# Products of 512 columns in place of two of 256, in the first superblock and the single feature tile of an MLP

## The chip, the cores and the metric

The kernel runs on one core of a Trainium2 chip. The metric is the device time of one execution in microseconds (us). The kernel before has a median of 372.47 us over three runs.

## The reference

One block of a network on x of shape 2048 x 512 (float32), with six modulation rows made from a condition vector c:

```python
mod = (silu(c) @ w_mod).reshape(6, 512)
sa, ca, ga, sb, cb, gb = mod
h = layernorm(x) * (1 + ca) + sa
x = x + ga * irfft2(rfft2(h) * (w_r + 1j * w_i))
h = layernorm(x) * (1 + cb) + sb
act = mish(h @ w1 + b1)              # w1: 512 x 1376
x = x + gb * (act @ w2)              # w2: 1376 x 512
```

## The kernel before

The Fourier filter is done first, as products with matrices of the transform: phase 1 forward (L258, L303 to L305, to 50 us), phase 2 with the filter (L528 to L597, to 90 us), and phase 3, the inverse, in 16 steps, each a `p3_col` (L830 and L831) and a `p3_row` (L840, with its add to x in L843), from 90.4 to 150 us. The weights of the MLP are prepared beside it, and the MLP starts at 133 us, while the last rows are added.

The MLP takes the 2048 rows in four superblocks `i` of 512, each made of two blocks `b` of 256. The 1376 features are five tiles of 256 (`t` = 1 to 5) and a single tile of 96 (`t` = 0, `FL` = 96). A float32 operand is split into a high and a low part, so that one product is three products of the list `TERMS` (high by high, high by low, low by high). `up` (L942) multiplies a block of the first weights, 2 x 2 blocks `A11` to `A22` to a tile, by an input block `B11` to `B22` (`Bkj`: contraction half k, row block j of the superblock); ScalarE evicts the result with Mish. In superblocks 1 to 3 the products are those of a scheme of seven products for 2 x 2 blocks (`PRODUCTS`), which needs sums of the blocks (`sum_w1`, L747, split by `split_w1`, L726 and L727). In superblock 0, the `PLAIN` one, they are the eight direct products, each of 6 instructions of 256 columns. `up_single` (L991) is the first product of the single tile, `down` the second product (L1041 for t = 0, L1045 for the others), `halves` splits the results for it (L877 on ScalarE, L878 on VectorE), `last_down` (L1057) is the end of the last block. `load_w1` (L716) loads both halves of a tile's first weights, `split_in` (L821, L822) splits an input block, `sum_w2` (L874) and `split_w2` (L877, L878) prepare the second weights, `mod_second` (L619) loads a piece of the modulation weights and `mod_column` (L165) sums it on VectorE.

The split input blocks live in tiles called slots: B11 and B21 in tiles of their own, B12 and B22 in a tile `hcr` in the space (tag `cr`) of a constant of the inverse transform, free after the last `p3_col`.

From phase 3 on every step stands in a plan with a key, and the plan is run in the order of a table of numbers, `ORDER`, in which the steps are named by their rank by key. Each engine takes its instructions in that order, and waits at the head of its queue; DMAs go out from SP's queue in the same way.

Of the kernel before, what the change touches and what calls it, by code (L numbers as in the profile page):

```python
# [82 lines left out]
def tile_spectral_block(ctx: ExitStack, tc: tile.TileContext, x_d, w1_d, b1_d, w2_d,  # L83
# [614 lines left out]
    odd = [pm.tile([P, 512], F32, name=f"odd{i}") for i in range(4)]  # L698
    slots = {b: pm.tile([P, 2, 2, 256], F32R, name=f"h{b}") for b in ("B11", "B21")}
# [206 lines left out]
    def hold(b, t):  # L906
        raw[b, t] = next(turn[b % 2])
        return raw[b, t]
# [18 lines left out]
    def up(i, t, j):  # L927
        a, b = j if (i, t) in PLAIN else PRODUCTS[j]
        w, h = ring[t, a], slots[b]
        if (i, t) in PLAIN:  # L930
            at, half = plain_place(t, int(a[1]) - 1, int(b[2]) - 1)
            if (i, t, at) not in ups:
                ups[i, t, at] = bank("AD"[at])
            o = ups[i, t, at][:, 256 * half:256 * half + 256]
            first, last = a[2] == "1" and half == 0, a[2] == "2"
        else:
            o = region(i, t, j)
            first, last = j in (1, 5), True
        n = 0
        for p, q in TERMS:  # L940
            for k in range(2):
                nc.tensor.matmul(o, w[:, p, k, :], h[:, q, k, :], start=(first and n == 0), stop=(last and n == 5),  # L942
                                 skip_group_check=True)
                n += 1
# [39 lines left out]
    def up_single(i, u):  # L984
        if u == 0:
            ups[i, 0] = bank("D")
        s = u // 2
        o = ups[i, 0][:FL, 256 * s:256 * s + 256]
        for m in range(6 * (u % 2), 6 * (u % 2) + 6):
            (p, q), k = TERMS[m // 4], m % 4  # L990
            nc.tensor.matmul(o, w1s[:, p, k, :], slots[f"B{k // 2 + 1}{s + 1}"][:, q, k % 2, :],  # L991
                             start=(u == 0 and m == 0), stop=(m == 11), skip_group_check=True)
# [32 lines left out]
    def order(b, t):  # L1025
        if t == 0:
            return [(n, half, d) for n, half in ((1, 1), (2, 0)) for d in range(2)]
# [4 lines left out]
    def down(b, t, c):  # L1032
# [5 lines left out]
        for i, (p, q) in enumerate(TERMS):  # L1038
            if t == 0:
                n, half, d = piece  # L1040
                nc.tensor.matmul(out_ps[b][n][:, 256 * d:256 * d + 256], a[p][:FL, half],  # L1041
                                 w2[0][q][:FL, 256 * d:256 * d + 256], start=False, stop=False, skip_group_check=True)
# [133 lines left out]
    def late_slots():  # L1176
        cr = big.tile([P, 2, 2, 2, 256], F32R, name="hcr", tag="cr")
        slots["B12"], slots["B22"] = cr[:, 0], cr[:, 1]

    plan.at(-0.95, late_slots)  # L1180
# [17 lines left out]
    first_odd = odd[1]  # L1198

    def odd_space():  # L1200
        odd[:] = [buf("g1"), buf("g1")] + odd
# [281 lines left out]
```

## Time and profile before

| | |
|---|---|
| time, median of three runs (lowest to highest) | 372.47 us (372.26 to 372.69) |
| the profiled execution | 372.4 us |
| its span, first to last instruction | 370.5 us |
| mean granted TensorE clock | 0.997 |
| PE busy, matmuls | 363.6 us (98%), 2884 |
| VectorE busy | 309.9 us (84%) |
| ScalarE busy | 253.6 us (68%) |
| GpSimd busy | 64.8 us (17%) |

The profiled execution's own time is 1.9 us above its span, which is what lies around the instructions. Matmuls are pipelined, so the duration of one (283 ns for 256 columns) is longer than the interval at which they follow one another; a cost is read from the start of one to the start of the next.

### The profile page before, as it was taken

Reading aid. Unit: us, or ns where it says so; the run is one execution under the profiler, and the core shown is the slowest. Engines: PE = TensorE matmul, PEld = TensorE weight load, DVE = VectorE, ACT = ScalarE, POOL = GpSimd, SP = SyncE. Lnnn points to the kernel's source line nnn. Section 1 sums busy time; section 2 is a strip of 40 time slices with the busy share of each in tenths; the row PEclk is TensorE's granted clock in tenths of the full one; section 3 lists DMA queues with packets and bytes.
Section 4 is the critical chain, followed back from the end, with each engine's and each line's share of the span. In section 5 each row is a group of like instructions: output and inputs, shape, how many; then the busy total and the mean of one; then the engine's idle time right before and its main releaser. Section 6 shows DMA issues by size and latency. Waiting matters only on the chain.

```text
span 370.5 us, 8169 instructions
## 1 busy us (share of the span) xinstructions
PE 363.6 (98%) x2884; PEld 348.6 (94%) x2884; DVE 309.9 (84%) x760; ACT 253.6 (68%) x553; POOL 64.8 (17%) x102
## 2 busy tenths in 40 slices
PE   8999999998999999999999999999999999999995
PEld 8989977777999999999999999999999999999994
DVE  1898967888898899999898868996768978867896
ACT  1698879996557789789575778765686744555750
POOL 0478738786000000000001000000000000000000
PEclk9999999999999999999999999999999999999998
DMA  7999998777624656856978699775996797936032
GB/s 233 380 340 350 346 389 264 239 177 288 230 85 143 227 193 226 284 178 222 316 237 219 199 282 271 238 211 168 291 303 224 196 306 227 296 121 176 15 58 113
DMA packets 50888, 85.79 MB, mean 232 GB/s; under 512 B 7169, under 2 KB 18529, under 8 KB 50593
## 3 DMA queue, kind: packets, MB, share of 16 engines
q1 hardware_dynamic: 47680, 74.65, 60.2%
q10 hardware_dynamic: 2160, 6.95, 6.0%
q0 software_dynamic: 1008, 3.67, 5.9%
q8 instruction: 23, 0.38, 0.4%
q14 instruction: 17, 0.13, 0.1%
HBM read 66.12 MB, written 15.47 MB: 220 GB/s over the span
## 4 chain that ended last, share of the span: by engine, by line
PE 84%; DVE 7%; ACT 5%; issue 2%; ACTq 1%; POOL 0%; DVEq 0%
PE bank L942 28%; PE bank L1045 24%; PE bank L830 4%; PE bank L840 4%; PE bank L831 4%; PE bank L258 4%; PE bank L991 3%; PE bank L303 3%; PE bank L1041 3%; ACT buf L580 1%; PE bank L314 1%; PE bank L305 1%; PE bank L304 1%; ACT buf L579 1%; ACT d L441 1%
## 5 line engine op out<-in xcount | busy, mean ns | idle before, releaser
L1097 POOL DMA_DIRECT2D x<-modr x7 | 6.2, 888 | 260.2 <-DVE st L172 104.5
L942 PE MATMUL bank<-hT,wr 128*128 128x256 f32 x360 | 51.7, 283 | 0.0
L942 PEld LDWEIGHTS bank<-hT,wr 128*128 128x128 f32 x360 | 46.9, 192 | 0.1
L942 PE MATMUL bank<-hB,wr 128*128 128x256 f32 x300 | 43.4, 284 | 0.0
L942 PEld LDWEIGHTS bank<-hB,wr 128*128 128x128 f32 x300 | 39.1, 191 | 0.0
L1045 PE MATMUL bank<-w2a,ah 128*128 128x256 f32 x161 | 35.3, 283 | 0.0
L878 DVE TENSOR_TENSOR al<-buf,ah 128x512 fp32r<-128x512 f32 (+1 forms) x45 | 29.7, 666 | 4.6 <-ACT ah L877 4.5
L1045 PE MATMUL bank<-w2b,ah 128*128 128x256 f32 x147 | 32.3, 283 | 0.0
L877 ACT CAST ah<-buf 128x512 fp32r<-128x512 f32 (+1 forms) x45 | 26.9, 602 | 5.6 <-PE bank L1045 3.2
L942 PE MATMUL bank<-hcr,wr 128*128 128x256 f32 x210 | 30.0, 283 | 0.0
L942 PEld LDWEIGHTS bank<-hcr,wr 128*128 128x128 f32 x210 | 27.2, 192 | 0.0
L1045 PEld LDWEIGHTS bank<-w2a,ah 128*128 128x128 f32 x161 | 26.8, 192 | 0.0
L830 PE MATMUL bank<-kc,d 128*128 128x128 f32 x128 | 24.9, 276 | 0.5 <-ACT d L441 0.5
L831 PE MATMUL bank<-kc,d 128*128 128x128 f32 x128 | 24.7, 275 | 0.0
L1045 PEld LDWEIGHTS bank<-w2b,ah 128*128 128x128 f32 x147 | 24.6, 191 | 0.0
L1045 PE MATMUL bank<-w,ah 128*128 128x256 f32 x112 | 22.0, 286 | 0.0
L172 DVE BATCH_NORM_STATS2 st<-x 128x6 f32<-128x512 f32 x32 | 21.9, 685 | 0.0
L303 PE MATMUL bank<-buf,mring 128*128 128x512 f32 x48 | 20.6, 430 | 0.2 <-DVE buf L296 0.2
L830 PEld LDWEIGHTS bank<-kc,d 128*128 128x128 f32 x128 | 19.4, 192 | 0.7 <-ACT d L441 0.7
L831 PEld LDWEIGHTS bank<-kc,d 128*128 128x128 f32 x128 | 19.4, 192 | 0.0
L597 PEld LDWEIGHTS bank<-kv,a_sb 128*128 128x128 f32 x126 | 15.4, 191 | 2.7 <-issue 2.2
L833 ACT COPY buf<-bank 128x512 f32<-128x512 f32 x16 | 9.3, 583 | 12.5 <-PE bank L831 12.5
(295 smaller groups left out, 1099.1 us busy)
## 6 DMA issues: line engine op xcount, KB each, us to landing
wr<-w_S SPq DMA_DIRECT2D x60, 256.0 KB, 3.7
wr<-w_A SPq DMA_DIRECT2D x45, 256.0 KB, 4.1
w_S<-hT SPq DMA_DIRECT2D x20, 256.0 KB, 2.0
x<-in_A_x_dram SPq DMA_DIRECT2D x16, 256.0 KB, 5.1
xring<-in_x_t_dram SPq DMA_DIRECT2D x16, 256.0 KB, 5.0
w_A<-wr SPq DMA_DIRECT2D x15, 256.0 KB, 2.6
x<-modr POOLq DMA_DIRECT2D x7, 512.0 KB, 5.6
out_dram<-x SPq DMA_DIRECT2D x7, 512.0 KB, 3.8
```

The source lines that it names most:

```text
L172: nc.vector.bn_stats(t, x[:, n, :])
L258: nc.tensor.matmul(pgv[:, j], data(j), krs[:, j, :].rearrange("p (c q) -> p c q", c=2), start=True, stop=True)
L303: nc.tensor.matmul(pa, m[:, a, 0:128], g, start=(i == 0), stop=False)
L597: nc.tensor.matmul(pd[:, i * P:(i + 1) * P], y[:, i * P:(i + 1) * P], kv[:, 0:128], start=True, stop=True)
L830: nc.tensor.matmul(o, dj[:, 0:128], kc[0][:, n, :], start=True, stop=False)
L831: nc.tensor.matmul(o, dj[:, 64:192], kc[1][:, n, :], start=False, stop=True)
L840: nc.tensor.matmul(px[:, j * P:(j + 1) * P], e[:, j * P:(j + 1) * P], kiv[:, j, :], start=True, stop=True)
L877: nc.scalar.copy(h, r)
L878: nc.vector.tensor_tensor(l, r, plain(h), op=ALU.subtract)
L942: nc.tensor.matmul(o, w[:, p, k, :], h[:, q, k, :], start=(first and n == 0), stop=(last and n == 5), skip_group_check=True)
L991: nc.tensor.matmul(o, w1s[:, p, k, :], slots[f"B{k // 2 + 1}{s + 1}"][:, q, k % 2, :], start=(u == 0 and m == 0), stop=(m == 11), skip_gro ...
L1045: nc.tensor.matmul(out_ps[b][n][:, 256 * half:256 * half + 256], a[p][:, e], w2[t][q][:, r], start=(t == 1 and half == 0 and i == 0), stop ...
```

## The change

In superblock 0, the tiles t = 2 to 5 are multiplied by a weight block with both row blocks at once: three instructions of 512 columns for one half of the contraction of a weight block (`b` in `up` is that half), where there were two times three of 256. The moving operand is then two runs of 256 columns, from the new paired tiles `sides`, which hold Bk1 and Bk2 side by side. The single tile does the same in `up_single`, in all four superblocks, and its second product (`down` with t = 0, blocks 0 to 6) writes the 512 output columns with one instruction. B12 and B22 thus move out of `hcr` into `sides`; four of the tiles for results of odd blocks (`odd`) move into the space `cr` instead. `ORDER` is written anew (1155 steps where there were 1170).

```diff
 ORDER = (
-    "3 1 0 2 5 16 21 52 6 15 7 32 8 10 4 12 17 13 11 14 73 24 19 38 47 26 9 22 75 62 23 71 27 20 69 118 18 25 29 "
...
+    "3-4 1-2 16 0 21 15 9 71 5 73 32 75 80 7 10 12 14 8 17 13 82 26 19 6 38 47 11 22 124 23-24 85 20 18 29 51 27 62 "
...
-    odd = [pm.tile([P, 512], F32, name=f"odd{i}") for i in range(4)]
-    slots = {b: pm.tile([P, 2, 2, 256], F32R, name=f"h{b}") for b in ("B11", "B21")}
+    odd = []
+    sides = [pm.tile([P, 2, 2, 2, 256], F32R, name=f"hB{k}") for k in (1, 2)]
+    slots = {f"B{k + 1}{s + 1}": sides[k][:, s] for k in range(2) for s in range(2)}
...
     def hold(b, t):
-        raw[b, t] = next(turn[b % 2])
+        n = next(turn[b % 2])
+        raw[b, t] = odd[n if b % 2 else 3] if b % 2 or n < 0 else (even[2], even[1], even[0], scb)[n]
         return raw[b, t]
...
     def up(i, t, j):
         a, b = j if (i, t) in PLAIN else PRODUCTS[j]
+        if (i, t) in PLAIN and t > 1:
+            f = int(a[1]) - 1
+            if (i, t, f) not in ups:
+                ups[i, t, f] = bank("AD"[f])
+            for n, (p, q) in enumerate(TERMS):
+                nc.tensor.matmul(ups[i, t, f], ring[t, a][:, p, b, :], sides[int(a[2]) - 1][:, :, q, b, :],
+                                 start=(a[2] == "1" and b == 0 and n == 0), stop=(a[2] == "2" and b == 1 and n == 2),
+                                 skip_group_check=True)
+            return
...
     def up_single(i, u):
         if u == 0:
             ups[i, 0] = bank("D")
-        s = u // 2
-        o = ups[i, 0][:FL, 256 * s:256 * s + 256]
-        for m in range(6 * (u % 2), 6 * (u % 2) + 6):
-            (p, q), k = TERMS[m // 4], m % 4
-            nc.tensor.matmul(o, w1s[:, p, k, :], slots[f"B{k // 2 + 1}{s + 1}"][:, q, k % 2, :],
-                             start=(u == 0 and m == 0), stop=(m == 11), skip_group_check=True)
+        for p, q in TERMS:
+            nc.tensor.matmul(ups[i, 0][:FL], w1s[:, p, u, :], sides[u // 2][:, :, q, u % 2, :],
+                             start=(u == 0 and p + q == 0), stop=(u == 3 and p == 1), skip_group_check=True)
...
         if t == 0:
-            return [(n, half, d) for n, half in ((1, 1), (2, 0)) for d in range(2)]
+            return [(1, 1), (2, 0)]
...
             if t == 0:
-                n, half, d = piece
-                nc.tensor.matmul(out_ps[b][n][:, 256 * d:256 * d + 256], a[p][:FL, half],
-                                 w2[0][q][:FL, 256 * d:256 * d + 256], start=False, stop=False, skip_group_check=True)
+                n, half = piece
+                nc.tensor.matmul(out_ps[b][n], a[p][:FL, half], w2[0][q][:FL], start=False, stop=False,
+                                 skip_group_check=True)
...
-    def late_slots():
-        cr = big.tile([P, 2, 2, 2, 256], F32R, name="hcr", tag="cr")
-        slots["B12"], slots["B22"] = cr[:, 0], cr[:, 1]
-
-    plan.at(-0.95, late_slots)
...
-    first_odd = odd[1]
-
     def odd_space():
-        odd[:] = [buf("g1"), buf("g1")] + odd
+        late = big.tile([P, 4, 512], F32, name="odd", tag="cr")
+        odd[:] = [buf("g1"), buf("g1")] + [late[:, i] for i in range(4)]
...
-    BY_WEIGHT = pairs("111", "112", "121", "122", "211", "212", "221", "222")
+    BY_WEIGHT = [(a, k) for a in ("A11", "A12", "A21", "A22") for k in range(2)]
...
-            for c in range(n):
-                plan.at(key + 0.5 * c, down, b, t, c)
-            key += 0.5 * n
+                plan.at(key + (0.5 if t else 1) * c, down, b, t, c)
+            key += 0.5 * n if t else 2
```

The code above the changed functions is one line shorter now, so L942's place for the direct products is L952 for t = 1 and L935 for t = 2 to 5, and L840's is unchanged.

TensorE's queue at the start of the MLP before (`hB_1287` and `hB_1288` are B11 and B21, `hcr` is B12 or B22, `wr` a weight block, L840 a `p3_row`):

```order
L942 MATMUL bank<-hB_1287,wr 128x256 x6
L942 MATMUL bank<-hB_1288,wr 128x256 x6
L840 MATMUL bank<-kiv,buf 128x128 x4
L942 MATMUL bank<-hB_1287,wr 128x256 x6
L942 MATMUL bank<-hcr,wr 128x256 x12
L942 MATMUL bank<-hB_1287,wr 128x256 x12
L942 MATMUL bank<-hB_1288,wr 128x256 x6
L942 MATMUL bank<-hcr,wr 128x256 x6
L942 MATMUL bank<-hB_1288,wr 128x256 x6
L942 MATMUL bank<-hcr,wr 128x256 x24
```

The same place after (`hB_1283` holds B11 and B12, `hB_1284` B21 and B22):

```order
L952 MATMUL bank<-hB_1283,wr 128x256 x6
L952 MATMUL bank<-hB_1284,wr 128x256 x6
L952 MATMUL bank<-hB_1283,wr 128x256 x6
L952 MATMUL bank<-hB_1284,wr 128x256 x6
L952 MATMUL bank<-hB_1283,wr 128x256 x6
L840 MATMUL bank<-kiv,buf 128x128 x4
L935 MATMUL bank<-hB_1283,wr 128x512 x3
L952 MATMUL bank<-hB_1284,wr 128x256 x6
```

Of t = 1 the order goes A11 B11, A12 B21, A21 B11, A22 B21, A11 B12, A12 B22; the first product with B22 is at the start of the 24 in the last row before, and is the last row after.

VectorE's queue at the start of phase 3, between the sums of the second weights (L874) and the first norms, before (`w_1241` and `w_1242` hold the second weights of t = 1, `modr` their sums, `hT_1358` the loaded first weights of t = 1):

```order
L165 SCALAR_TENSOR_TENSOR buf,cols<-buf,bank 128x512
L878 TENSOR_TENSOR w_1242<-buf,w_1241 128x256
L878 TENSOR_TENSOR w_1242<-buf,w_1241 128x512
L843 TENSOR_TENSOR x<-x,bank 128x512
L878 TENSOR_TENSOR w_1242<-modr,w_1241 128x1024
L172 BN_STATS st<-x 128x6
L173 BN_AGGR mv<-st 128x2
L843 TENSOR_TENSOR x<-x,bank 128x512
```

And after (`hT_1292` is the loaded weights, `hT_1321` their sums, `hT_1322` the split sums):

```order
L878 TENSOR_TENSOR w_1242<-buf,w_1241 128x256
L878 TENSOR_TENSOR w_1242<-buf,w_1241 128x512
L747 TENSOR_TENSOR hT_1321<-hT_1292 128x256 x2
L878 TENSOR_TENSOR w_1242<-modr,w_1241 128x1024
L727 TENSOR_TENSOR hT_1322<-hT_1321,hT_1322 128x256 x2
L843 TENSOR_TENSOR x<-x,bank 128x512 x2
L171 BN_STATS st<-x 128x6
```

Two sums of first weights and the splits of their low parts now stand ahead of the first two adds of phase 3, and the third column sum of the modulation (L165, now L164) has moved behind them.

SP's queue of DMAs there, before:

```order
L866 DMA buf<-in_B_w_dram 128x512 x2
L619 DMA buf<-in_w_mod_dram 128x512 x5
L716 DMA hT_1358<-in_B_w_dram 128x4x256
L716 DMA hT_1381<-in_B_w_dram 128x4x256
L866 DMA buf<-in_B_w_dram 128x512 x2
```

And after:

```order
L866 DMA buf<-in_B_w_dram 128x512 x2
L618 DMA buf<-in_w_mod_dram 128x512 x2
L716 DMA hT_1292<-in_B_w_dram 128x4x256
L618 DMA buf<-in_w_mod_dram 128x512 x2
L757 DMA buf<-in_B_w_dram 128x4x96
```

The first load of the first weights went ahead of three of the five pieces of the modulation's, and the second load of them behind.

More of the change, by code (lines that the diff above doesn't have):

```diff
@@ L1196, in tile_spectral_block @@
             plan.at(key + scale * at, sum_w1, t, a, step)
-    first_odd = odd[1]
     def odd_space():
-        odd[:] = [buf("g1"), buf("g1")] + odd
+        late = big.tile([P, 4, 512], F32, name="odd", tag="cr")
+        odd[:] = [buf("g1"), buf("g1")] + [late[:, i] for i in range(4)]
     plan.at(1.6, odd_space)
-    turn = turns([even[2], first_odd, even[1], even[0], scb], [even[2], even[1], even[0], scb]), turns([], odd)
+    turn = turns([0, -1, 1, 2, 3], range(4)), turns([], range(6))
     def pairs(*ab):
@@ L1231, in tile_spectral_block @@
         if (i, t) in PLAIN:
-            f, e = int(j[0][1]) - 1, int(j[1][2]) - 1
-            at, half = plain_place(t, f, e)
-            if j[0][2] == "2" and half:
+            f, e = int(j[0][1]) - 1, int(j[1][2]) - 1 if t == 1 else j[1]
+            if j[0][2] == "2" and (f if t == 1 else e):
                 for h in range(2):
@@ L1291, in tile_spectral_block @@
                 plan.at(u + s + 2, scale_turned, b, g)
-        split_at, sum_at = (((35.2, 36.2, 37.2, 38, 37.5, 38.7, 40, 40.5), (35.4, 38.2, 36.5, 39.2)) if i == 1 else
+        split_at, sum_at = (((36.6, 36.8, 38.3, 38, 37.5, 38.7, 40, 40.5), (36.9, 38.2, 37, 39.2)) if i == 1 else
                             ((33.3, 33.8, 37.3, 38.3, 39.3, 40.3, 41.3, 42.3), (34.65, 35.15, 36.65, 38.15)))
```

85 rows, old and new, of the table ORDER are left out of this document.

## The prediction, made before the changed kernel was run

> **What bounds the kernel now.** I read the page first, for the engines' shares, then the busy time by stretches, the waits of TensorE, the chain that ended last, and the timeline of single engines where the change touches them.
>
> ```profile
> PE 363.6 (98%) x2884; PEld 348.6 (94%) x2884; DVE 309.9 (84%) x760; ACT 253.6 (68%) x553; POOL 64.8 (17%) x102
> PE bank L942 28%; PE bank L1045 24%; PE bank L830 4%; PE bank L840 4%; PE bank L831 4%; PE bank L258 4%; PE bank L991 3%; PE bank L303 3%; PE bank L1041 3%; ACT buf L580 1%; PE bank L314 1%; PE bank L305 1%; PE bank L304 1%; ACT buf L579 1%; ACT d L441 1%
> ```
>
> TensorE is busy for 98% of the span, and the products of the MLP (L942, L1045, L991, L1041) are most of the chain that ended last. The busy time by stretches (columns: the stretch, its length, PE, PEld, DVE, ACT, POOL, granted clock, DMA share, GB/s) says it stage by stage:
>
> ```profile
> 96.00:133.30 37.30, 37.30 (x337) 37.30 (x336) 34.84 (x86) 24.82 (x55) 0.00 (x0) 1.00 0.52 177
> 133.30:180.00 46.70, 46.70 (x395) 46.70 (x394) 43.78 (x117) 39.16 (x89) 0.00 (x0) 1.00 0.69 235
> 100.00:340.00 240.00, 240.00 (x2027) 239.98 (x2026) 204.98 (x513) 164.46 (x352) 5.37 (x6) 1.00 0.73 226
> ```
>
> From 100 to 340 us TensorE never stops, at a granted clock of 1.00. VectorE is at 93% and 94% in the two early stretches, so it is the engine that may become late. The waits of TensorE (us in total, times, longest), the one wait of its weight loads at the end, and the last wait of VectorE for TensorE:
>
> ```profile
> PE bank L830 <- ACT d L441: 0.5, 1, 0.5
> 356.84 0.19 PEld L1057 LDWEIGHTS bank<-w2hi,al 128*128 128x128 f32 x1 [0.24 <-DVE al L878]
> 344.86 0.42 DVE L978 TENSOR_TENSOR buf<-buf,bank 128x256 f32<-128x256 f32 x1 [0.47 <-PE bank L942]
> ```
>
> The first is at 90.4 us, at the start of the inverse transform; the second comes when nearly all is done. VectorE itself last waits for TensorE at 344.86, so an earlier TensorE pulls the tail with it: time taken out of TensorE's queue before that point is time off the end, unless something else is late.
>
> **The change part by part: what is saved.** 186 pairs of products of 256 columns become single products of 512: in the first superblock t=2 to 5 have 4 x 8 units of 6 products, 192, now 96 (96 pairs); the single tile's first product has 4 x 24, now 4 x 12 (48 pairs); its second has 7 blocks x 12, now 6 (42 pairs). The columns streamed stay the same; what goes is a fixed part for each product. Its size is the interval from one product's start to the next, in the chain (start, length, what) and in the timeline at the end, where products of 512 already run:
>
> ```profile
> 135.87 12.22 PE bank L942 x102
> 205.38 1.44 PE bank L1041 x12
> 220.84 1.42 PE bank L991 x12
> 360.75 0.63 PE L1057 MATMUL bank<-w2b,ah 128*128 128x512 f32 x2
> 361.22 0.39 PE L1057 MATMUL bank<-w2b,al 128*128 128x512 f32 x1
> 361.45 0.63 PE L1057 MATMUL bank<-w2b,ah 128*128 128x512 f32 x2
> 361.91 0.39 PE L1057 MATMUL bank<-w2b,al 128*128 128x512 f32 x1
> 362.14 0.39 PE L1057 MATMUL bank<-w2c,ah 128*128 128x512 f32 x1
> ```
>
> A product of 256 takes 12.22 / 102 = 120 ns in the first product, 1.44 / 12 = 120 in the second, 1.42 / 12 = 118 in the single tile's first. Six of 512 go from 360.75 to 362.14: 1.39 / 6 = 231 or 232 ns; I take 231. A pair saves 240 - 231 = 9 ns, or 236.5 - 231 = 5.5 with the single tile's weights of 96 columns. The sum: 96 x 9 = 0.86 us, 42 x 9 = 0.38, 48 x 5.5 = 0.26, together 1.5 us. All of it lies on the path, since TensorE is never idle there, but for some 3 pairs that follow 344.86 (0.03 us).
>
> The bounds of this come from phase 1, where both sizes alternate:
>
> ```profile
> 26.51 0.40 PE L303 MATMUL bank<-buf,mring 128*128 128x512 f32 x1
> 26.75 0.28 PE L304 MATMUL bank<-buf,mring 128*128 128x256 f32 x1
> 26.86 0.28 PE L305 MATMUL bank<-buf,mring 128*128 128x256 f32 x1
> 26.98 0.40 PE L303 MATMUL bank<-buf,mring 128*128 128x512 f32 x1
> ```
>
> Here 512 columns take 0.24 and two of 256 take 0.23: no saving at all to the second digit. That is the low end, 0: the same columns stream, and nothing in these rows makes one long product dearer than two short ones. The high end is 186 x 11 = 2.0 us, if the 512 runs at 229 (361.45, 361.91 and 362.14 lie 0.23 to a product apart, read to the second digit). I take 9, since those rows have the MLP's own tiles and the other kind of row has weights in another order. The fixed part left by these rows is 240 - 231 = 9 ns for each product. The Trainium skill, TensorE: Matmul & The Clock Gate, section Back-to-back issue gap, gives an isolated gap of columns / 2.4 plus 2.5 ns, 215.8 for 512 and 109.2 for 256; the trace has 231 and 120, so it does not agree in size. By that rule a pair would save 2.6 ns and the whole change 0.5 us.
>
> **What is moved.** The content of every other engine's queue stays: the same casts, subtractions and transfers, in another order. Three places decide whether TensorE runs into a wait.
>
> First, the low part of B22 (L822), which VectorE makes just before TensorE multiplies with it:
>
> ```profile
> 139.67 0.69 DVE L822 TENSOR_TENSOR hcr<-even,hcr 128x512 fp32r<-128x512 f32 x1
> 140.28 0.42 DVE L727 TENSOR_TENSOR hT<-wsum,hT 128x256 fp32r<-128x256 f32 x1
> 92.65 0.42 DVE L874 TENSOR_TENSOR modr<-buf 128x256 f32<-128x256 f32 x1
> 92.99 0.42 DVE L874 TENSOR_TENSOR modr<-buf,modr 128x256 f32<-128x256 f32 x1
> ```
>
> The two L874 rows show an operation on 256 columns at 0.34 from start to start (92.65 to 92.99), the first two rows one on 512 at 0.61. The low part ends at 139.67 + 0.69 = 140.36; TensorE gets to that block 48 products after 135.87, at 141.62, 1.26 us later. After the change TensorE gets there with 30 products of 256 fewer in front (3.60 us) and 3 of 512 more (0.69): 2.91 us sooner. VectorE has less ahead of it too: three differences of weights (L747) and two of L874 move behind it, 0.34 each, 1.70; one split of 256 and one of 512 of the second weights move behind, 0.34 + 0.61; a column sum for the gate moves ahead (+0.61) and one p3_row add behind (-0.61), both on 512. Together 2.65 us. The slack becomes 1.26 - (2.91 - 2.65) = 1.0 us: still no wait.
>
> Second, the start of the inverse transform. The load of the first pair of weight blocks (L716, 512 KB) moves in SP's queue ahead of three loads of the modulation (L619), and what VectorE makes of it moves ahead of the first two p3_row adds (L843): two differences (L747) and two splits (L727). Before:
>
> ```profile
> 84.46 11.24 SPq L619 DMA_DIRECT2D buf<-in_w_mod_dram  x5
> 95.89 0.93 SPq L716 DMA_DIRECT2D hT<-in_B_w_dram  x2
> hT<-in_B_w_dram SPq DMA_DIRECT2D x5, 512.0 KB, 4.2
> wm<-in_w_mod_dram SPq DMA_DIRECT2D x7, 256.0 KB, 8.8
> 89.18 0.68 DVE L165 SCALAR_TENSOR_TENSOR wm<-wm,bank 128x512 f32<-128x512 f32 x1
> 94.65 0.69 DVE L165 SCALAR_TENSOR_TENSOR buf<-buf,bank 128x512 f32<-128x512 f32 x1 [1.24 <-DMA buf<-in_w_mod_dram]
> 95.26 1.14 DVE L878 TENSOR_TENSOR w<-buf,w 128x256 fp32r<-128x256 f32 x2
> 96.32 0.68 DVE L843 TENSOR_TENSOR x<-x,bank 128x512 f32<-128x512 f32 x1
> 96.92 1.22 DVE L878 TENSOR_TENSOR w<-modr,w 128x1024 fp32r<-128x1024 f32 x1
> 98.06 0.69 DVE L172 BATCH_NORM_STATS2 st<-x 128x6 f32<-128x512 f32 x1
> 99.43 0.83 PE L840 MATMUL bank<-kiv,buf 128*128 128x128 f32 x6
> ```
>
> The load can go out once VectorE's second sum of wm is done, at 89.18 + 0.68 = 89.86, so about 89.9, and lands 4.2 us later by the median of its kind, at 94.1. VectorE, which now doesn't stand 1.24 us for the third modulation block, goes on from 92.99 + 0.34 = 93.33 with the splits of 256 and 512, 0.34 + 0.61, to 94.3, or 94.6 where it waits for ScalarE's casts, as it does between 95.26 and 96.32; then 0.67 (two differences), 1.14 (the split of 1024, 96.92 to 98.06), 0.67 (two splits of 256) and 0.60 (the add, 96.32 to 96.92) take the add to 97.7. TensorE wants the bank it frees for its third p3_row at 99.43. Slack 1.7 us: no wait; behind this add stand only row 1's add and the sums of the norm.
>
> Third, the tiles. B12 and B22 now share tiles with B11 and B21 and need not await the end of the inverse transform, and four tiles for odd blocks take over the old space; the first use of these comes with results of t=2, which TensorE makes after the last p3_col:
>
> ```profile
> 133.32 0.22 PE bank L831 x2
> ```
>
> That only relaxes the early part, and I cost it at nothing; its cover is the 12 us of products from 135.87 on, which follow in either kernel. If a first eviction did stand in ScalarE's queue there, its bank would be late for TensorE, and 0.04 of the chances below is kept for that. In superblocks 1 to 3 the steps keep their neighbours; TensorE loses 24 pairs' worth, 0.2 us, in each against VectorE, which has more than 30 us of idle time in 100 to 340. So I add nothing.
>
> The profiled execution took 372.4 us for a span of 370.5; the runs' median is 372.47. The sum is 370.5 - 1.5 = 369.0 of span, 1.9 around it, and 370.9 by the profiled time, 371.0 by the median. I say **371.0 us**. 0.2%, about what a measurement of this kernel can tell from no change, is 0.75 us.
>
> **The rivals.**
>
> *The load is late (slower).* At the start of the inverse transform the load of 512 KB could take the 8.8 us that the wm rows show in the same queue: it lands at 98.7, VectorE's queue stands, the add ends 98.7 + 0.67 + 1.14 + 0.67 + 0.60 = 101.8, and TensorE, wanting the bank at 99.43, waits 2.4 us: 371.0 + 2.4 = 373.4. It decides from a landing later than 99.43 - 3.08 = 96.35, 6.4 us after the issue. For it: the wm rows. Against it: all five loads of this very kind, median 4.2. Chance 0.12.
>
> *VectorE takes the gain at B22 (same).* If VectorE's queue is later by 1.0 us plus what is gained, TensorE waits for the low part of B22 and the end stays where VectorE puts it: 372.3. For it: 94% of VectorE in that stretch. Against it: the count above, with 1.0 us to spare. Chance 0.08.
>
> *The pairs save nothing (same).* If the moving operand in two runs of 256 costs as two products, or a product's fixed part is as in phase 1 (0.24 against 0.23), the time stays at 372.4. No row of before has a moving operand in two runs; for it stand the phase 1 rows, against it those of L1057. By that rule of the Trainium skill it would be 372.0. Chance 0.08.
>
> **How the numbers follow.** The forecast has 0.68: 371.0, or 370.4 to 371.7 with 2.0 us and 0.75 us for the gain. The late load has 0.12, and 0.04 I keep for a wait of its size elsewhere, such as that of the evictions for the new tiles; the two rivals in between 0.08 + 0.08 = 0.16. Faster by over 0.2% is the forecast's: 0.68. Within 0.2%: the two rivals, 0.16. Slower: 0.12 + 0.04 = 0.16. For 8 in 10 the forecast's own range and the rivals in between don't quite do, as some of the forecast's 0.68 lies outside 370.4 to 371.7; so the range reaches on to the late load's price: 370.4 to 373.4.
>
> **What would show it.** Right: TensorE's busy time shorter by about 1.5 us with 186 fewer products; products of 512 in L935 and in the single tile's lines at 231 ns from start to start; no new wait of PE between 91 and 356 us. The late load would show as a wait of PE L840 <- DVE x L843 near 99 us, with VectorE idle for a transfer to hT just before; the B22 rival as PE waiting for DVE L822 near 139; the third as 240 ns between products of 512. The forecast is wrong if the busy time of PE falls by under 0.75 us, or if it falls as said and idle time of the same size appears.

## The result and the profile after

The changed kernel is slower, by 1%:

| | before | after |
|---|---|---|
| median of five runs (lowest to highest) | 372.53 us (372.26 to 372.69) | 376.07 us (375.12 to 377.41) |
| ratio, 95% interval | | 1.0098 (1.0071 to 1.0126) |
| profiled execution | 372.4 us | 375.33 us |
| its span | 370.5 us | 373.2 us |
| matmuls | 2884 | 2698 |

The profiled execution of the changed kernel is one of the faster of its five.

The page of the changed kernel, busy time and the chain that ended last:

```profile
PE 362.7 (97%) x2698; PEld 338.0 (91%) x2698; DVE 309.5 (83%) x760; ACT 252.0 (68%) x553; POOL 64.9 (17%) x102
PE 88%; DVE 6%; DMA 3%; issue 1%; ACT 0%; SPq 0%; DVEq 0%; ACTq 0%
```

186 products are gone, yet the chain now has 3% of DMA in it, where the page of before names no DMA among the engines of its chain. The waits of TensorE name it (us in total, times, longest); no such row stood before:

```profile
PE bank L952 <- DMA wr<-w_S: 3.3, 1, 3.3
```

TensorE waited once, for 3.3 us, for a weight block fetched into `wr` (L952 makes the products of superblocks 1 to 3 too, not only those of t = 1). The chain around that moment (start, length, what):

```profile
254.04 5.71 DMA wr<-w_S
259.75 0.14 issue
259.89 1.37 PE bank L952 x6
261.26 1.28 PE bank L1052 x6
262.54 1.24 PE bank L1048 x3
```

The fetch was issued at 254.04 and landed 5.71 us later. SP's queue says why it went so late: its timeline after, and one of its waits between 240 and 262 us.

```profile
244.75 0.32 SPq L723 DMA_DIRECT2D wr<-w_S  x1
249.88 4.06 SPq L790 DMA_DIRECT2D turned<-x  x4
254.04 1.21 SPq L723 DMA_DIRECT2D wr<-w_S  x1
SPq L790 <- DVE x L784: 4.7, 1, 4.7
```

From about 245 us SP stood with `turn_out` of rows 12 and 13 (L790) at the head of its queue, 4.7 us, for a transpose of VectorE (L784). Its four DMAs then took 4.06 us to go out, and only then came the fetch of t=3 S3, which TensorE wanted at 256.6 (259.89 less its wait of 3.3). Before the change the same four DMAs stood behind that fetch and four more (S3 is the second `w_S` of the first row, A11 and A22 are the second row, S4 and S2 the third):

```profile
246.05 1.76 SPq L723 DMA_DIRECT2D wr<-w_S  x2
248.57 2.48 SPq L723 DMA_DIRECT2D wr<-w_A  x2
252.53 1.26 SPq L723 DMA_DIRECT2D wr<-w_S  x2
256.14 1.77 SPq L790 DMA_DIRECT2D turned<-x  x4
```

The loss is larger than the wait. The rows after it are slow: 6 products of 256 in 1.37 and in 1.28 us, 228 and 213 ns each where 120 is usual. The granted clock in the stretches before, in and after the wait (the column before the last two):

```profile
256.00:259.89 3.89, 0.60 (x6) 0.42 (x5) 1.06 (x5) 0.00 (x0) 0.00 (x0) 1.00 0.94 241
259.89:263.80 3.91, 3.91 (x17) 3.63 (x18) 0.89 (x2) 1.44 (x3) 0.00 (x0) 0.56 1.02 366
263.80:268.00 4.20, 4.20 (x34) 4.07 (x34) 3.08 (x7) 2.75 (x7) 0.00 (x0) 1.00 1.06 374
```

For 3.91 us after the wait the clock was 0.56 of full speed, then 1.00 again: 3.91 x 0.44 = 1.7 us of work lost on top of 3.3. So the stretch from the first product of phase 3 to the last group of the MLP's first product (h @ w1), before and after,

```profile
90.40 0.49 PE L830 MATMUL bank<-kc,d 128*128 128x128 f32 x2 [0.46 <-ACT d L441]
343.93 0.89 PE L942 MATMUL bank<-hcr,wr 128*128 128x256 f32 x6
89.73 0.49 PE L830 MATMUL bank<-kc,d 128*128 128x128 f32 x2 [0.46 <-ACT d L440]
346.69 0.89 PE L952 MATMUL bank<-hB,wr 128*128 128x256 f32 x6
```

was 343.93 - 90.40 = 253.53 us and is 346.69 - 89.73 = 256.96: 3.4 us more, which is 3.3 + 1.7 lost, so that 1.6 was gained. Phases 1 and 2 were 0.7 us shorter in this execution, so the span is longer by 2.7 alone; the medians differ by 3.5.

### The profile page after: what moved, and what is told of

It is laid out like the page before. It is cut to its first block, busy times and chain, and to the rows that moved or that the text cites. A ratio compares the mean times of both kernels' runs of the same rounds, so it can differ in the third digit from the quotient of the medians.

```text
span 373.2 us, 7800 instructions
## 1 busy us (share of the span) xinstructions
PE 362.7 (97%) x2698; PEld 338.0 (91%) x2698; DVE 309.5 (83%) x760; ACT 252.0 (68%) x553; POOL 64.9 (17%) x102
## 4 chain that ended last, share of the span: by engine, by line
PE 88%; DVE 6%; DMA 3%; issue 1%; ACT 0%; SPq 0%; DVEq 0%; ACTq 0%
PE bank L1052 23%; PE bank L952 22%; PE bank L935 6%; PE bank L830 4%; PE bank L840 4%; PE bank L831 4%; PE bank L547 4%; PE bank L257 4%; PE bank L998 3%; PE bank L596 3%; PE bank L1048 3%; PE bank L302 3%; PE bank L527 2%; DMA wr<-w_S 2%; PE bank L304 1%; PE bank L303 1%
## 5 line engine op out<-in xcount | busy, mean ns | idle before, releaser
L952 PE MATMUL bank<-hT,wr 128*128 128x256 f32 x360 | 51.6, 285 | 3.3 <-DMA wr<-w_S 3.3
L1104 POOL DMA_DIRECT2D x<-modr x7 | 6.2, 888 | 263.6 <-DVE al L878 178.7
L952 PEld LDWEIGHTS bank<-hT,wr 128*128 128x128 f32 x360 | 47.2, 193 | 3.9 <-issue 3.5
L952 PE MATMUL bank<-hB,wr 128*128 128x256 f32 x318 | 44.8, 283 | 0.0
L952 PEld LDWEIGHTS bank<-hB,wr 128*128 128x128 f32 x318 | 41.6, 191 | 0.8
L935 PE MATMUL bank<-hB,wr 128*128 128x512 f32 x96 | 25.2, 395 | 0.0
L877 ACT CAST ah<-odd 128x384 fp32r<-128x384 f32 (+1 forms) x13 | 6.8, 524 | 24.0 <-PE bank L1052 19.9
L935 PEld LDWEIGHTS bank<-hB,wr 128*128 128x128 f32 x96 | 17.1, 189 | 2.9
```

The source lines that it names most:

```text
L877: nc.scalar.copy(h, r)
L935: nc.tensor.matmul(ups[i, t, f], ring[t, a][:, p, b, :], sides[int(a[2]) - 1][:, :, q, b, :], start=(a[2] == "1" and b == 0 and n == 0), s ...
```

## The experiments

All times below are medians on one chip, where the kernel before had 372.9 us beside the first four kernels and 372.7 beside the other four.

The two theories for the late fetch: **A**, the order in SP's queue (the fetch stands behind DMAs that wait for VectorE); **B**, the transfer itself is slow at that time, beside GpSimd's accumulating DMA (L1104, 512 KB), which goes out at 251.50.

**e1: the fetches first.** The edit in the order of the steps of the changed kernel (`...` stands for steps of other kinds):

```diff
-turn_out (12, 2)
 ...
 fetch_w1 (3, 'S3')
 ...
 fetch_w1 (4, 'A11')
 ...
 fetch_w1 (3, 'A22')
 ...
 fetch_w1 (3, 'S4')
 ...
 fetch_w1 (4, 'S2')
+turn_out (12, 2)
```

> The changed kernel with one step moved: the four DMAs that write the turned rows of the last superblock (L790, turn_out of 12) go behind five fetches of first weights (t=3 S3, t=4 A11, t=3 A22, S4, t=4 S2), as they stand before the change. Theory A (SP's queue stands at the turned rows for VectorE's transposes, and the fetch of S3 behind them comes late): TensorE's wait of 3.3 us at 259.9 is gone, the time falls from 376.1 to 371 to 372, under the kernel before. Theory B (the transfer of S3 is slow by itself, since the DMA engines carry GpSimd's accumulating DMA then): the wait stays at over 2 us and the time at 375 to 376.

Measured: 373.02 us, ratio to before 1.0011 (0.9993 to 1.0030). The wait for `wr` is gone, which is A's mark. But the kernel is level with before, not under it, as another wait came up. TensorE's waits, and SP's and ScalarE's timeline of e1:

```profile
PE bank L952 <- ACT buf L801: 1.1, 1, 1.1
262.00 0.43 SPq L1113 DMA_DIRECT2D out_dram<-x  x1
262.79 3.38 SPq L790 DMA_DIRECT2D turned<-x  x4
266.76 0.54 SPq L796 DMA_DIRECT2D buf<-turned  x1
272.79 2.08 ACT L801 ACTIVATE buf<-buf,cols 128x256 f32<-128x256 f32 x4 [2.94 <-DMA buf<-turned]
```

ScalarE stood 2.94 us for a read of the turned rows, issued behind the store of block 2 and the second group of turned rows, with evictions queued behind it that TensorE needed.

**e2: GpSimd's DMA later.** SP's order stays; one step is moved, VectorE's product L1103 and the accumulating DMA that GpSimd issues with it:

```diff
-residual (2, 1)
 ...
 turn_in ('B11', 12, 0)
+residual (2, 1)
```

> The changed kernel with one other step moved: the residual of block 2 (VectorE's product L1103 and GpSimd's accumulating DMA at 251.5 us) goes behind the read of the turned rows, some 35 steps later; SP's queue keeps its order. Theory A alone: SP still stands until 249.9 for the transposes, the wait stays at about 3 us, 375 to 376. Theory B (GpSimd's DMA slows the issues on SP between 250 and 257 us, 4.06 us for four where others take 1.8, and the transfers): the wait shrinks by about 2 us to 1, 373 to 374.

Measured: 377.4 us, ratio 1.0132 (1.0101 to 1.0163), slower than either theory said. The waits of TensorE and of SP, and the timelines of e2:

```profile
PE bank L952 <- ACT ah L877: 4.3, 1, 4.3
SPq L1113 <- DMA x<-modr: 7.6, 1, 7.6
249.63 3.03 SPq L790 DMA_DIRECT2D turned<-x  x4
252.75 0.38 SPq L723 DMA_DIRECT2D wr<-w_S  x1
256.18 0.88 PE L952 MATMUL bank<-hT,wr 128*128 128x256 f32 x6
265.81 0.34 SPq L1113 DMA_DIRECT2D out_dram<-x  x1
```

SP still stood for the transposes until 249.63, but the four DMAs took 3.03 us, the fetch went out at 252.75, and TensorE began the products of S3 at 256.18 without a wait: the fetch landed within 3.4 us, where it took 5.71 beside GpSimd's DMA. So the order in SP's queue puts the fetch at the edge, and an issue slower by 1.0 us and a landing slower by 2.3 us or more pushed it over. That fits B in part; but VectorE's product moved together with GpSimd's DMA, and this run does not separate the two. The kernel lost elsewhere: the store of block 2 (L1113) waits in SP's queue for GpSimd's DMA, now until 265.81, with the second turned rows, their reads and the next fetches behind it, and ScalarE stood 4.8 us for such a read and TensorE 4.3 us behind it, until 277.10; in the 4.00 us from 277.00 the granted clock was 0.57. It is the same mechanism at another head of the same queue.

**e3: pairs of 256 again, on e1.** Each product of 512 made as before, in the order of e1:

```diff
-nc.tensor.matmul(ups[i, t, f], ring[t, a][:, p, b, :], sides[int(a[2]) - 1][:, :, q, b, :], ...)
+for s in range(2):
+    nc.tensor.matmul(ups[i, t, f][:, 256 * s:256 * s + 256], ring[t, a][:, p, b, :], sides[int(a[2]) - 1][:, s, q, b, :], ...)
```

and likewise in `up_single` and `down`.

> e1_fetch_first with every new product of 512 columns made again as two of 256, in the same order of steps (186 products more, as many as before the change). If a pair saves 9 ns (5.5 in the single tile's first product), as forecast: 1.5 us slower than e1_fetch_first, about the time of the kernel before. If it saves nothing: the same time as e1_fetch_first. If the fixed part is 2.6 ns: 0.5 us slower.

Measured: 375.23 us, ratio to before 1.0063 (1.0041 to 1.0084), 2.2 us above e1. Its trace has waits of 1.7 us for `wr` where e1 had 1.1 for ScalarE, 0.6 more, so the pairs account for at most 1.8 of the 2.4 us by which its span (372.6) is longer than e1's (370.2).

**e4: the kernel before with its turned rows first.** The same five fetches put behind `turn_out (12, 2)`; nothing of the change is in it.

> The kernel before with the same five fetches put behind the turned rows of the last superblock (L790, turn_out of 12). Theory A: SP stands for the transposes until 256 us with the fetches behind it, TensorE waits 3 to 6 us near 260 us for wr, 375 to 378. Theory B: about 372.5 to 373.5.

Measured: 378.33 us, ratio 1.0148 (1.0125 to 1.0171): A, in the kernel that has none of the products of 512. The chain of e4 and the granted clock after the wait:

```profile
258.75 4.17 DMA wr<-w_A
262.96 1.65 PE bank L942 x6
PE bank L942 <- DMA wr<-w_A: 4.8, 1, 4.8
262.96:267.00 4.04, 4.04 (x21) 4.04 (x22) 0.71 (x1) 1.43 (x3) 0.00 (x0) 0.59 1.00 281
```

The wait is 4.8 us and the clock 0.59 for 4 us after it, 1.7 us more; together 6.5, for a span of 377.3 against 370.5.

**e5: e1 with the store later.** The store of block 2 goes behind the four reads of turned rows, as before the change:

```diff
-store (2,)
 ...
 turn_in ('B22', 14, 1)
+store (2,)
```

> e1_fetch_first with a second step moved: the store of block 2's rows (L1113, 512 KB, at 262 us in SP's queue ahead of the second group of turned rows) goes behind the four reads of turned rows, as before the change. Theory: the wait of 1.1 us that e1_fetch_first has left at 274.9 (ScalarE stands for a read of turned rows, issued at 266.8 and landed 6.0 us later) goes too, no wait of TensorE over 0.3 us after 91 us is left, and the span falls by 1.1 us to 369.1, 1.2 to 1.5 us under the kernel before. Rival: the next late transfer takes its place and the time stays that of e1_fetch_first.

Measured: 371.74 us, ratio to before 0.9975 (0.9959 to 0.9992): faster than both kernels, 0.3 to 1.5 us under the kernel before by that interval, 1.0 by the medians. Its waits of TensorE are those of phases 1 and 2 alone, the last at the start of phase 3:

```profile
PE bank L830 <- ACT d L440: 0.5, 1, 0.5
90.24 0.49 PE L830 MATMUL bank<-kc,d 128*128 128x128 f32 x2 [0.46 <-ACT d L440]
342.20 0.90 PE L952 MATMUL bank<-hB,wr 128*128 128x256 f32 x6
```

In its profiled execution, one of the faster ones (370.84 us), the same stretch takes 342.20 - 90.24 = 251.96 us, 1.57 less than before.

**e6: only S3 first.** As e1, with `turn_out (12, 2)` behind `fetch_w1 (3, 'S3')` alone.

> The changed kernel with the turned rows (turn_out of 12) behind one fetch only, that of t=3 S3. If that fetch alone was late: the wait of 3.3 us is gone, the four other fetches come in time, and the time is that of e1_fetch_first or a little less. If the fetches behind the turned rows are late too: a wait of 1 to 3 us on wr moves to t=4 A11 or t=3 A22, 374 to 375.

Measured: 373.27 us, ratio 1.0013 (0.9993 to 1.0033). The wait moved to the next fetch, as the second expectation said, though the time is under its 374 to 375: 1.3 us for `wr`, t=4 A11, which went out at 253.38 and took 7.20 us to land, and another 0.5 us for a block of `w_S`.

```profile
PE bank L952 <- DMA wr<-w_A: 1.3, 1, 1.3
253.38 7.20 DMA wr<-w_A
```

**e7: pairs of 256 again, on e5.**

> e5_fetch_first_store_later with every product of 512 of the change made again as two of 256. The trace of the changed kernel has 512 columns at 227 ns in L935 and 230 to 232 in the single tile's lines, so pairs cost 96 x 12.5 + 42 x 9 + 48 x 6 ns = 1.9 us more in span, if no wait comes in; 1.5 by the forecast's sizes; 0 if pairs save nothing.

Measured: 374.69 us, ratio to before 1.0050 (1.0034 to 1.0067), 2.95 us above e5. The stretch from phase 3 to the last group of the first product is 346.15 - 90.56 = 255.59 us, 3.6 more than e5's. In it TensorE is idle for 1.37 + 0.20 us (first two rows), 1.4 of them a wait for `wr` that e5 doesn't have, against 0.07 in e5 (last row): 1.5 us. The rest, 2.1, is an upper bound for the pairs, since what a wait costs beyond its idle time is in it too.

```profile
200.00:300.00 100.00, 98.63 (x823) 98.46 (x822) 80.32 (x197) 68.77 (x142) 2.59 (x3) 1.00 0.81 245
300.00:350.00 50.00, 49.80 (x414) 49.47 (x412) 37.99 (x95) 25.24 (x54) 1.72 (x2) 1.00 0.64 190
200.00:300.00 100.00, 99.93 (x790) 97.19 (x789) 81.38 (x197) 69.41 (x143) 2.60 (x3) 1.00 0.82 245
```

With the products of before, the new order is slower than the old one.

**e8: e6 with the store later.**

> e6_only_s3_first with the store of block 2 behind the reads of turned rows, as in e5. Theory: the best of these orders, 1.2 to 1.9 us under the kernel before, without a wait of TensorE over 0.3 us after 91 us. Rival: turned rows at the head of the queue still make a fetch late, 373 to 375.

Measured: 372.25 us, ratio 0.9982 (0.9966 to 0.9998). The store's place gains here too (1.0 us against e6), but the wait for t=4 A11 (1.2 us) stays, so the theory failed. Its median is 0.5 us above e5's; the two intervals overlap, so which of the two orders is better is not shown.

## Why the prediction was wrong

**The saving was right.** Forecast 1.5 us. The intervals of the changed kernel (timeline rows of L935 with the product that follows, the chain's row of the single tile's first product, and three products of its second with the one that follows):

```profile
142.31 7.74 PE L935 MATMUL bank<-hB,wr 128*128 128x512 f32 x33
149.89 0.40 PE L1052 MATMUL bank<-w,ah 128*128 128x256 f32 x2
275.25 1.39 PE bank L998 x6
264.33 0.40 PE L1048 MATMUL bank<-w2b,ah 96*128 96x512 f32 x1
265.03 0.87 PE L952 MATMUL bank<-hT,wr 128*128 128x256 f32 x6
```

From start to start a product of 512 takes (149.89 - 142.31) / 33 = 230 ns in L935 (I took 231), 1.39 / 6 = 232 in the single tile's first product and 0.70 / 3 = 233 in its second: 96 x 10 + 42 x 7 + 48 x 4.5 ns = 1.5 us. The 227 ns in the expectation of e7 come from a row of the chain, 7.50 us for the same 33, which counts the first of them only from the end of the product ahead of it; the 1.9 us there are too high for that reason. e5 shows 1.57 us against before in the profiled stretch and 1.0 in the medians; e3 against e1 and e7 against e5 have at most 1.8 and 2.1. The two runs of 256 in the moving operand cost nothing that these rows show. By the rule of the Trainium skill weighed above (TensorE: Matmul & The Clock Gate, Back-to-back issue gap) it would have been 0.5; the trace stays with its own rows, 120 and 230 to 233.

**The three places that I looked at held.** VectorE's work there, SP's load and TensorE's use, after the change:

```profile
89.35 0.38 SPq L716 DMA_DIRECT2D hT<-in_B_w_dram  x1
93.87 0.75 DVE L747 TENSOR_TENSOR hT<-hT 128x256 f32<-128x256 f32 x2
96.98 1.28 DVE L843 TENSOR_TENSOR x<-x,bank 128x512 f32<-128x512 f32 x2
98.77 1.06 PE L840 MATMUL bank<-kiv,buf 128*128 128x128 f32 x8
135.37 0.68 DVE L822 TENSOR_TENSOR hB<-even,hB 128x512 fp32r<-128x512 f32 x1
138.12 2.15 PE bank L952 x18
```

The load went out at 89.35 and VectorE used it at 93.87, so it landed in 4.5 us at most (forecast 4.2, with 6.4 as the point of decision). The first p3_row add was done at 97.6 (96.98 + 0.60) and TensorE came at 98.77: 1.2 us of slack, forecast 1.7. The low part of B22 was done at 136.05, its product began at 138.12: 2.1 us, forecast 1.0. The tiles in the new space made no wait.

**The step that failed** is the sentence "In superblocks 1 to 3 the steps keep their neighbours ... So I add nothing". They don't: `turn_out (12, 2)` went ahead of five fetches and the store of block 2 ahead of three reads of turned rows, and I followed SP's queue at the start of phase 3 only. The term that I put at nothing measured 5.0 us (3.3 of wait and 1.7 of slow clock): the profiled forecast of 370.9, less the 0.7 of phases 1 and 2, plus 5.0, is 375.2, against 375.33 measured. VectorE's 30 us of idle time, which I named as cover, is no cover for a DMA that stands behind another DMA in SP's queue. e1 shows the first of these moves worth 3 us, e5 the second 1.3, and e4 that the first one costs the kernel before 5.4. The slower rival was of this kind, a late transfer behind a moved one, but at another place; the 0.04 kept for "a wait of its size elsewhere" is what came, but at twice its price, so that the time lies above the range. Of the signs of being wrong, the last came: the busy time of TensorE fell, by 0.9 us (363.6 to 362.7) with the 1.7 of slow clock in it, and idle time appeared, 3.3 us, more than was saved.

**A long wait costs more than its length.** The rival's 2.4 us, and with it the range's end at 373.4, counted a wait at its length. The wait of 3.3 cost 5.0, as the clock went to 0.56 for 3.9 us after it; in e4 4.8 cost 6.5. In e7 the granted clock after a wait of 1.4 us stayed at 1.00; what a wait between 1.4 and 3.3 us does, such as the rival's 2.4, no run shows:

```profile
276.73:280.70 3.97, 3.97 (x33) 3.97 (x34) 2.95 (x8) 2.80 (x6) 0.00 (x0) 1.00 1.05 400
```

The Trainium skill has a rule for this in TensorE: Matmul & The Clock Gate, Part 1: The HAM clock gate: after an idle window of about 3.4 us the clock is half, until TensorE has been busy for about as long. The traces agree with it: after idle times of 3.3, 4.3 and 4.8 us the clock was 0.56, 0.57 and 0.59 over about 4 us, after 1.4 it was 1.00; the 3.3 lies at the edge of the page's figure.

**What stays open:** why the four DMAs of turned rows take 4.1 to 4.8 us to go out in after, e1, e3, e5 and e7, 2.7 to 3.0 in e2, e6 and e8, and 1.8 in before and e4. GpSimd's DMA goes out within 1.7 us of their start in all but e2, before and e4, which fits B only in part.

## What to carry to other kernels

When an order is written anew, compare every in-order queue from end to end, the DMA queue first: for each transfer that an engine waits for, list what now stands ahead of it and what that waits for. A saving that is spread thin over TensorE (4 to 10 ns in each of 186 pairs) is lost to one late fetch of 256 KB. And price a long wait of TensorE (3.3 us and more here) with the slow clock that follows it.

## What the runs showed of the hardware

A fetch of 256 KB, behind the turned rows in the same stretch of the program, landed in 3.4 us or less, in 5.7 or in 7.2, in three orders of the same steps (S3 in e2 and after, A11 in e6); the shortest is the one with GpSimd's accumulating DMA of 512 KB not yet out. A median of landings over the whole run (3.8 us for those of `w_S` and 4.1 for those of `w_A` in the changed kernel) is no price for a transfer in a busy stretch.
